# Column halves for the large loads of a half chunk, and a new set of priorities, in a planned recurrence and gated feed-forward kernel

## The chip, the core and the metric

One core of a Trainium2 chip. The metric is the device time of one execution in microseconds, the median of several runs. Engines: TensorE (PE in the profile, its weight loads PEld), VectorE (DVE), ScalarE (ACT), GpSimd (POOL) and SyncE (SP), which issues every transfer of this kernel through one queue, in order. Sixteen DMA engines move the bytes.

## What is computed

Two parts, one after the other: a recurrence over 768 tokens for 4 batches and 8 heads of width 40, and a gated feed-forward layer on its output.

```python
for t in range(S):                                   # S = 768
    y[:, :, t] = einsum('bhd,bhde->bhe', r_t, state)
    Sa = einsum('bhde,bhe->bhd', state, a_t)
    state = state * w_t - einsum('bhd,bhe->bhde', Sa, b_t) + einsum('bhd,bhe->bhde', v_t, k_t)
x = y as 3072 rows of 320
out = ((x @ w_a) * (x @ w_b)) @ w_out                # w_a, w_b 320 x 1536, w_out 1536 x 320
```

## The kernel before

The tokens are cut into 12 chunks of 64 (C), and the 32 pairs of batch and head into two halves (c = 0, 1) of 16; a "half chunk" is one c of one chunk n. For each chunk the recurrence becomes matrix work:

- `prep(n, c, v)` (one half chunk, independent of the state). It loads W (decays) and BA, a row of 1536 numbers: columns 0 to 1023 hold b and k (BK), columns 1024 to 1535 hold a (A). DVE makes running products of the decays (two scans into Q, the reciprocal d between them), multiplies BK and A by them, PE makes the scores (`at<-BA`) and transposes BK (`at<-ident,BA`), ACT stores the scores of one kind into AB, DVE those of the other into TK. TK, A and part of Q go to a scratch row in memory, `un_d[q]`, from which `main` reads them.
- `lanes(g, v, halved)` (a group of one or two chunks: 0; 1 and 2; 3 and 4; ...). A triangular solve on DVE: transpose N, then steps that each are a product Yt and a sum Y, then two transposes, TC and T. For the first two groups `halved` shortens the steps (14 pairs instead of 30), and `join` on PE and ACT puts the halves together. `merge` makes of it the matrix T of each chunk.
- `main(n, v)` (the chain over the chunks). It loads ak and pt (both from `un_d`), SV (v by tokens) and RV (r in its first half, v in its second, by channels), then runs a chain on PE with ACT and DVE between: `r_` (`at<-SV,ak`), `u_` and `ut_` (`at<-RH,T`, `at<-T,RH`), `s_` (`at<-SV,bn`, the new state ST), `g_` (`at<-rv`, masked by DVE into G: `G<-at,tri`), `y_` (`at<-rv,SD`, `at<-G,bn`). `pack` lays the result out as xk, the input of the feed-forward layer.
- The feed-forward weights come as 64-bit words. They are cut into 12 slices of 128 columns, each of three pieces (w_a, w_b, w_out). `decode` turns a piece into a high and a low part by a chain of small steps that alternates between ACT, DVE and POOL, through two raw buffers and one pair of temporaries, so the pieces go one after the other. The slices 0 to 5 (F1) are decoded while the first chunks run; the `sc` entry of WG starts them after the scores of half chunk 1. `unit` is one slice on one chunk: 16 matmuls `ab<-xk,wt`, a product g by ACT and DVE, 6 matmuls `po<-wo`. Slices 0 to 5 are done chunk by chunk beside the recurrence, slices 6 to 11 at the end, on two chunks at a time (`at<-xk,wt`, 512 columns).

What sets the order: every step is recorded in a `Plan` with its engine, a length, what it reads and writes, and a priority v. `Plan.run` then lays the steps out in time by its own table of lengths, and at each point an engine takes, of the steps that could begin, the one with the smallest v. The instructions are issued in that order, and on the chip each engine runs its own in that order, waiting wherever an input is late. So priorities, lengths and dependencies set the order on every engine at once.

The priorities are simple sums. With rank the first chunk of a group:

```python
prep(n, c, rank[n] + PV + PV1 * (n - rank[n]) + 0.1 * c)
wv = [WV + WV1 * f if f < F1 else NS - 3 + 0.3 * (f - F1) for f in range(NSL)]
lanes(g, g[0] + LV if g[0] else LV0, halved)
join(n, x, n + MV);  merge(g, g[0] + MV);  main(n, n);  units of chunk n: n + UV + f / F1
```

Before: the preps of chunk 0 have -2.99 and -2.89, those of chunk 1 have -1.99 and -1.89, the solve of chunk 0 has -1.85 (LV0), and the weight slices 0 to 5 have -4.44 to -3.64. A transfer is a step of SP with a number of microseconds for its bytes; the plan also holds that a transfer is issued only when the eighth transfer before it has landed.

Of the kernel before, what the change touches and what calls it, by code (L numbers as in the profile page):

```python
# [23 lines left out]
C = 64  # L24
# [3 lines left out]
NP = 2  # L28
# [27 lines left out]
SMALLEST = 0.5 / (1.125 * 2.0 ** -15)  # L56
PV, PV1, LV, MV, UV, WV, WV1 = -2.99, 0.43, -0.68, -1.45, 1.44, -4.44, 0.16
LV0 = -1.85
LIMIT = 2.0 ** 8
# [274 lines left out]
def wkv_moe(ctx, tc, wd, ba, rvf, vn, pin, rv, wa, wb, wo, out):  # L334
# [310 lines left out]
    def prep(n, c, v):  # L645
# [26 lines left out]
        load(lambda: (W, wd[n, c]), n, [], [kW], 0.75)  # L672
        load(lambda: (BA, ba[n, c]), n, [], [kBK, kA], 2.5)

# [236 lines left out]
    def main(n, v):  # L911
# [9 lines left out]
        for c, q in enumerate(qs):  # L921
            vc = v + 0.1 * c
            pl.dma(lambda q=q: nc.sync.dma_start(out=AK_[q % NU], in_=un_d[q][:, 0:AW]),
                   [("un", q, i) for i in (0, 1, 3, 4)] + begun(n), [kU[c]], 1.65, v=vc - 0.3)
            load_v(n, c, vc - 0.2)
            load(lambda c=c: (RV_[c].rearrange("p x m t -> p (x m t)"), rvf[n, c]), n, begun(n), [kRV[c]], 1.7, v=vc - 0.2)
            pl.dma(lambda q=q: nc.sync.dma_start(out=PT_[q % NU], in_=un_d[q][:, AW:]), [("un", q, 2)] + begun(n), [kP[c]], 0.85, v=vc - 0.1)
# [10 lines left out]
        def r_(ps=ps):  # L938
            for c in both:
                for i in range(4):  # L940
                    for gq in range(2):
                        for j in range(2):
                            k = mi(gq, i) * D
                            mul(bank(ps, c)[half(j), k:k + D], AK[c][:, gq, j, i], SV[:, c, gq, j, i])
        pl.op("PE", 1.86, r_, ["svs", *kV, *kU], [("r", n), "rh"], need=ps, work=2560, mode="cc", lat=0.1)
        for c in both:
# [65 lines left out]
        for c in both:  # L1012
            ps = Banks(2)

            def g_(c=c, ps=ps):
                for m in range(M):
                    for kind in range(2):
                        for gq in range(2):
                            l = RV_[c][hd(gq), 1, m] if kind else UT[hd(gq), c, m]
                            mul(bank(ps, gq)[half(gq ^ kind), m * C:(m + 1) * C], l, RV_[c][hd(gq), 0, m])  # L1020
            pl.op("PE", 0.98, g_, [("ut", 0), ("ut", 1), kRV[c]], [("gs", n, c), ("gm", c, 0), ("gm", c, 1)], need=ps, work=1280, mode="qq", lat=0.1, v=v + 0.1)
            for gq in range(2):
                pl.op("DVE", us(512), lambda c=c, gq=gq, ps=ps: nc.vector.tensor_mul(
                    out=G[:, c, gq].rearrange("p j i t -> p (j i) t"), in0=bank(ps, gq).rearrange("p (m t) -> p m t", t=C),
                    in1=tri[:, None, :].to_broadcast([P, M, C])), [("gs", n, c)],
                    [("gm", c, gq)] + ([("xf", 0, x) for x in range(4)] if c else ["x"]), free=[(ps, gq)], v=v + 0.1)
# [3 lines left out]
        def y_(ps=ps):  # L1030
# [8 lines left out]
            for c in both:  # L1039
                for gq in range(2):  # L1040
                    for i in range(4):
                        for j in range(2):
                            c0 = (c * 4 + i) * C
                            mul(bank(ps, gq)[hd(j), c0:c0 + C], BN[c][:, mi(gq, i), j], G[:, c, gq, j, i], not n, True)
        pl.op("PE", 2.9 if n else 2.1, y_, [("gm", c, x) for c in both for x in range(2)] + [*kBN, *kRV] + [("sd", c) for c in both],
              [("y", n), "x"], need=ps, work=6144, mode="qc" if n else "cc", lat=0.1, v=v + 0.2)
# [164 lines left out]
    class Later:  # L1211


        def __init__(self, s, i):
            self.s, self.i = s, i

    keys_a = ([(k, i) for k in ("U", "pt") for i in range(NU)] + [("bn", i, k) for i in range(NBN) for k in range(2)] + [("T", i, k) for i in range(NT) for k in range(3)]
              + [(k, c) for k in ("svv", "rv", "sd", "ut") for c in range(NP)] + ["svs", "rh", "st", "x"]
              + [("gm", c, x) for c in range(NP) for x in range(2)] + [("xf", 0, i) for i in range(4)] + ["judge"])
# [282 lines left out]
```

## Time and profile before

| | |
|---|---|
| median of 3 runs (lowest, highest) | 752.42 us (749.15, 755.53) |
| the profiled execution | 752.64 us |
| its span, first to last instruction | 750.9 us |
| granted TensorE clock, mean over the span | 0.916 |
| busy: PE, DVE, ACT, POOL | 673.7, 539.2, 400.8, 230.1 us |
| moved by the transfers | 117.11 MB in 68692 packets |

Busy time counts what an engine executes; issuing transfers and waiting on semaphores are not counted. The chain of waits is followed back from the last instruction, at each step to what released it. "issue" is time in which an engine waited for nothing that the profile shows. All work issued through the planner shows line 75, so groups are told apart by tiles. The clock is given as a share of 2.4 GHz: 1.00 is 2.4 GHz, 0.50 is 1.2 GHz.

### The profile page before, as it was taken

To read this page: it belongs to the slowest core of one execution; us is meant where nothing else is said; L and a number is where in the kernel's file an instruction comes from. 1 tells how busy PE (TensorE), PEld (TensorE's weight loads), DVE (VectorE), ACT (ScalarE), POOL (GpSimd) and SP (SyncE) were. 2 spreads that over 40 slices of the span, in tenths; PEclk is the share of its full clock that TensorE was granted. 3 is DMA by queue.
4 is the path that set the end of the run, shared out by engine and by line. 5 is a ranking of instruction groups with operands and counts; after the bars stand their busy time and mean duration, and the time that the engine had idled before them with its cause. 6 is when DMAs were issued, how large, how long until landed. Compare 5 with 4: busy or idle time off the path is not lost.

```text
span 750.9 us, 29601 instructions
## 1 busy us (share of the span) xinstructions
PE 673.7 (90%) x12997; PEld 619.3 (82%) x12997; DVE 539.2 (72%) x992; ACT 400.8 (53%) x898; POOL 230.1 (31%) x236
## 2 busy tenths in 40 slices
PE   5446765997999998999999999999999999999996
PEld 3435654897999988989899999899998888888886
DVE  8999998889688995999789998466374444322133
ACT  5547667475663575556746545586475344312221
POOL 5034444341001121211211111266375465522220
PEclk8556666598999998999999999999999999999998
DMA  7998698146685685667656617383841111000112
GB/s 221 316 294 247 162 297 237 50 129 203 195 263 171 200 263 167 184 200 201 217 167 183 204 40 207 100 225 114 256 133 52 43 39 38 3 1 4 67 71 75
DMA packets 68692, 117.11 MB, mean 156 GB/s; under 512 B 6796, under 2 KB 46764, under 8 KB 68556
## 3 DMA queue, kind: packets, MB, share of 16 engines
q1 hardware_dynamic: 68556, 115.14, 52.0%
q8 instruction: 104, 1.70, 1.0%
q14 instruction: 32, 0.26, 0.1%
HBM read 76.91 MB, written 32.80 MB: 146 GB/s over the span
## 4 chain that ended last, share of the span: by engine, by line
PE 79%; DVE 11%; issue 5%; DMA 3%; SPq 1%; POOL 1%; ACT 1%; DVEq 0%; POOLq 0%
PE at L75 41%; PE ab L75 24%; PE po L75 13%; DVE Q L75 2%; DVE Y L75 1%; DVE Yt L75 1%; DVE BA L75 1%; DMA ak<-un_d 1%; DMA wraw<-in_wb_dram 1%; DVE G L75 1%; DVE w_ex L75 1%; DMA wraw<-in_wo_dram 1%; SPq L75 1%; DVE TC L75 1%; DVE TK L75 1%
## 5 line engine op out<-in xcount | busy, mean ns | idle before, releaser
L75 PE MATMUL ab<-xk,wt 120*128 120x256 f32 x1216 | 171.0, 294 | 0.0
L75 PEld LDWEIGHTS ab<-xk,wt 120*128 120x128 f32 x1216 | 157.9, 198 | 2.8 <-issue 0.2
L75 PE MATMUL at<-xk,wt 120*128 120x512 f32 (+1 forms) x576 | 132.1, 381 | 0.0
L75 POOL TENSOR_TENSOR gl<-g,gh 128x256 fp32r<-128x256 f32 x66 | 59.4, 902 | 230.8 <-ACT gh L75 202.4
L75 PEld LDWEIGHTS at<-xk,wt 120*128 120x128 f32 x576 | 102.9, 188 | 19.1
L75 PE MATMUL po<-wo,gh 128*128 128x320 f32 x312 | 85.4, 324 | 0.7 <-issue 0.7
L75 DVE TENSOR_TENSOR m<-at,m 128x512 f32<-128x512 f32 x32 | 22.1, 691 | 85.3 <-PE at L75 83.1
L75 DVE TENSOR_TENSOR Yt<-Y,N 128x112 f32<-128x112 f32 (+22 forms) x173 | 70.1, 405 | 4.0
L75 DVE TENSOR_TENSOR Y<-Y,Yt 128x112 f32<-128x112 f32 (+22 forms) x173 | 65.3, 377 | 5.9
L75 POOL TENSOR_TENSOR w_mt<-w_mt,w_ex 120x384 f32<-120x384 f32 (+1 forms) x33 | 36.0, 1090 | 94.1 <-ACT w_mt L75 93.2
L75 POOL TENSOR_TENSOR m<-m,m 128x512 fp32r<-128x512 f32 x32 | 41.7, 1303 | 75.4 <-ACT m L75 75.2
L75 ACT COPY g<-ab 128x256 f32<-128x256 f32 x76 | 28.2, 371 | 62.0 <-PE ab L75 59.1
L75 PEld LDWEIGHTS po<-wo,gh 128*128 128x128 f32 x312 | 56.4, 191 | 2.5 <-issue 0.9
L75 DVE TENSOR_TENSOR g<-ab,g 128x256 f32<-128x256 f32 x76 | 31.7, 417 | 32.8 <-ACT g L75 32.5
L75 ACT CAST m<-m 128x512 fp32r<-128x512 f32 x32 | 19.9, 621 | 58.7 <-DVE m L75 57.0
L75 DVE TENSOR_TENSOR BA<-BA,Q 128x1024 f32<-128x1024 f32 (+1 forms) x48 | 48.9, 1038 | 0.1
L75 PE MATMUL po<-wo,gl 128*128 128x320 f32 x156 | 48.8, 313 | 0.0
L75 PE MATMUL at<-BA 64*64 64x64 f32 x1536 | 36.0, 252 | 12.4 <-issue 9.3
L75 PEld LDWEIGHTS at<-BA 64*64 64x64 f32 x1536 | 31.9, 163 | 16.2 <-issue 10.9
L75 ACT CAST gh<-g 128x256 fp32r<-128x256 f32 x80 | 32.4, 406 | 22.1 <-DVE g L75 20.2
L75 PE MATMUL at<-ident,BA 104*128 104x104 f32 x192 | 27.2, 285 | 15.6 <-DVE BA L75 7.8
L75 ACT ACTIVATE AB<-at 32x256 f32<-32x256 f32 (+1 forms) x72 | 32.4, 450 | 15.0 <-PE at L75 13.8
(122 smaller groups left out, 1363.5 us busy)
## 6 DMA issues: line engine op xcount, KB each, us to landing
BA<-in_ba_dram SPq DMA_DIRECT2D x22, 672.0 KB
ak<-un_d SPq DMA_DIRECT2D x24, 512.0 KB
rv<-in_rvf_dram SPq DMA_DIRECT2D x22, 448.0 KB
un_d<-Q SPq DMA_DIRECT2D x24, 260.0 KB
pt<-un_d SPq DMA_DIRECT2D x24, 260.0 KB
un_d<-BA SPq DMA_DIRECT2D x48, 128.0 KB
un_d<-TK SPq DMA_DIRECT2D x48, 128.0 KB
x_d<-G SPq DMA_DIRECT2D x12, 512.0 KB
```

The source lines that it names most:

```text
L75: r = fn(*args, **kwargs)
```

## The change

Three loads are issued as two transfers of half the columns or of the two parts (BA in 1024 and 512 columns, RV and ak in 512 and 512), each half with a key of its own in the plan, and eight priorities have new values.

```diff
-PV, PV1, LV, MV, UV, WV, WV1 = -2.99, 0.43, -0.68, -1.45, 1.44, -4.44, 0.16
-LV0 = -1.85
+PV, PV1, LV, MV, UV, WV, WV1 = -3.05, 0.55, -0.63, -1.25, 1.35, -4.72, -1.4
+LV0 = -4.93
...
-        load(lambda: (BA, ba[n, c]), n, [], [kBK, kA], 2.5)
+        load(lambda: (BA[:, 0:2 * M * C], ba[n, c][:, 0:2 * M * C]), n, [], [kBK], 1.67)
+        load(lambda: (BA[:, 2 * M * C:], ba[n, c][:, 2 * M * C:]), n, [], [kA], 0.83)
...
-            pl.dma(lambda q=q: nc.sync.dma_start(out=AK_[q % NU], in_=un_d[q][:, 0:AW]),
-                   [("un", q, i) for i in (0, 1, 3, 4)] + begun(n), [kU[c]], 1.65, v=vc - 0.3)
+            for g in range(2):
+                ag = slice(g * AW // 2, (g + 1) * AW // 2)
+                pl.dma(lambda q=q, ag=ag: nc.sync.dma_start(out=AK_[q % NU][:, ag], in_=un_d[q][:, ag]),
+                       [("un", q, i) for i in (0, 1, 3, 4)] + begun(n), [(*kU[c], g)], 0.83, v=vc - 0.3)
             load_v(n, c, vc - 0.2)
-            load(lambda c=c: (RV_[c].rearrange("p x m t -> p (x m t)"), rvf[n, c]), n, begun(n), [kRV[c]], 1.7, v=vc - 0.2)
+            for x in range(2):
+                load(lambda c=c, x=x: (RV_[c][:, x].rearrange("p m t -> p (m t)"), rvf[n, c][:, x * M * C:(x + 1) * M * C]),
+                     n, begun(n), [(*kRV[c], x)], 0.85, v=vc - 0.2)
...
-        pl.op("PE", 1.86, r_, ["svs", *kV, *kU], [("r", n), "rh"], need=ps, work=2560, mode="cc", lat=0.1)
+        pl.op("PE", 1.86, r_, ["svs", *kV, *((*k, g) for k in kU for g in range(2))], [("r", n), "rh"], need=ps, work=2560, mode="cc", lat=0.1)
...
-            pl.op("PE", 0.98, g_, [("ut", 0), ("ut", 1), kRV[c]], [("gs", n, c), ("gm", c, 0), ("gm", c, 1)], need=ps, work=1280, mode="qq", lat=0.1, v=v + 0.1)
+            pl.op("PE", 0.98, g_, [("ut", 0), ("ut", 1), (*kRV[c], 0), (*kRV[c], 1)], [("gs", n, c), ("gm", c, 0), ("gm", c, 1)], need=ps, work=1280, mode="qq", lat=0.1, v=v + 0.1)
...
-        pl.op("PE", 2.9 if n else 2.1, y_, [("gm", c, x) for c in both for x in range(2)] + [*kBN, *kRV] + [("sd", c) for c in both],
+        pl.op("PE", 2.9 if n else 2.1, y_, [("gm", c, x) for c in both for x in range(2)] + [*kBN, *((*k, 0) for k in kRV)] + [("sd", c) for c in both],
```

With the new values the solve of chunk 0 stands at -4.93, the preps of chunk 0 at -3.05 and -2.95, those of chunk 1 at -2.05 and -1.95, and the weight slices 0 to 5 at -4.72, -6.12 and so on down to -11.72. The raw buffers keep the pieces in their old order. The key of a's part lets the first half of an RV load (r, read by `g_` and `y_`) and the second (v, read by `g_` alone) come free at different steps.

What the change makes of the order, at three places.

VectorE at the start, from the second TK product of chunk 0 (`TK_182`; `Q_178`, `BA_179` belong to chunk 1, `w_mt` to the first weight piece, N, AB, Y and Yt to the solve of chunk 0). Before:

```order
L75 TENSOR_TENSOR TK_182<-at_63,tri 128x512
L75 SCALAR_TENSOR_TENSOR Q_178<-W_176,one 128x521
L75 RECIPROCAL d_183<-Q_178 128x8
L75 SCALAR_TENSOR_TENSOR Q_178<-W_176,d_183 128x520
L75 STREAM_TRANSPOSE N<-AB 128x32x32
L75 TENSOR_TENSOR AB<-AB,off 128x16x32
L75 TENSOR_TENSOR BA_179<-BA_179,Q_177 128x1024
L75 TENSOR_SCALAR w_mt_162<-wraw_159 120x384
L75 TENSOR_TENSOR BA_179<-BA_179,Q_177 128x512
L75 COPY Y<-N 128x2x15
```

and now:

```order
L75 TENSOR_TENSOR TK_182<-at_63,tri 128x512
L75 STREAM_TRANSPOSE N<-AB 128x32x32
L75 TENSOR_TENSOR AB<-AB,off 128x16x32
L75 COPY Y<-N 128x2x15
L75 TENSOR_TENSOR Yt<-Y,N 128x56
L75 TENSOR_TENSOR Y<-Y,Yt 128x2x2x14
```

The scans, the products of chunk 1 and all weight steps have left the solve; it runs through without a break, and the first weight step stands right behind its last transpose.

VectorE where the first chunk's chain reaches G (`ST` and `G<-at,tri` belong to main(0); Y and Yt now to the solve of chunks 1 and 2). Before:

```order
L75 TENSOR_TENSOR Yt<-Y,N 128x128
L75 TENSOR_TENSOR Y<-Y,Yt 128x2x8x8
L75 TENSOR_TENSOR ST<-at_66,pcs 128x8x40
L75 TENSOR_TENSOR ST<-at_65,pcs 128x8x40
L75 TENSOR_TENSOR Yt<-Y,N 128x126
L75 TENSOR_TENSOR Y<-Y,Yt 128x2x9x7
L75 TENSOR_TENSOR G<-at_64,tri 128x512
```

and now:

```order
L75 TENSOR_TENSOR ST<-at_63,pcs 128x8x40
L75 TENSOR_TENSOR ST<-at_65,pcs 128x8x40
L75 TENSOR_TENSOR AB<-AB,off 128x16x32
L75 TENSOR_SCALAR w_mt_162<-wraw_159 120x384
L75 TENSOR_TENSOR TK_181<-at_64,tri 128x512
L75 TENSOR_TENSOR G<-at_65,tri 128x512
L75 TENSOR_TENSOR BA_180<-BA_180,Q_178 128x512
L75 TENSOR_TENSOR G<-at_63,tri 128x512
L75 COPY Y<-N 128x2x15
```

Eight pairs of solve steps and the copy Y, which stood ahead of the first G, now stand behind the second; beside them one product of BA_180, one `w_mt`, two `w_ex` of each kind have moved behind G too.

TensorE between `g_` and `y_` of chunk 2 (`wt_224` is slice 0, `wt_226` slice 1, `wt_228` slice 2, `wt_234` and `wo_235` slice 5). Before:

```order
L75 MATMUL at_65<-rv_205 64x64
L75 MATMUL ab_68<-xk,wt_234 128x256 x8
L75 MATMUL ab_67<-xk,wt_224 128x256 x16
L75 MATMUL at_65<-rv_204,SD_210 40x64
L75 MATMUL at_66<-rv_204,SD_210 40x64
```

and now:

```order
L75 MATMUL at_65<-rv_205 64x64
L75 MATMUL ab_67<-xk,wt_228 128x256 x16
L75 MATMUL ab_68<-xk,wt_226 128x256 x8
L75 MATMUL po_69<-wo_235,gh_166 128x320
L75 MATMUL po_69<-wo_235,gl_168 128x320
L75 MATMUL po_69<-wo_235,gh_166 128x320
L75 MATMUL po_70<-wo_235,gh_166 128x320
L75 MATMUL po_70<-wo_235,gl_168 128x320
L75 MATMUL po_70<-wo_235,gh_166 128x320
L75 MATMUL at_65<-rv_204,SD_210 40x64
```

What moved is feed-forward work: counted from the start of the program to the `y_` of chunk 2, PE now has 136 `ab` matmuls, 36 `po` and 472 of the preps' matmuls, where it had 112, 30 and 440; the counts of the solves and of the main chain are the same. Up to the first `ab` the only difference is one set of 32 score matmuls that now stands ahead of it.

## Rows read from the trace of the kernel before

**Rows 1.** The page, part 1 and the clock line of part 2.

```profile
PE 673.7 (90%) x12997; PEld 619.3 (82%) x12997; DVE 539.2 (72%) x992; ACT 400.8 (53%) x898; POOL 230.1 (31%) x236
...
PEclk8556666598999998999999999999999999999998
```

**Rows 2.** Stages: length, busy PE, PEld, DVE, ACT, POOL; clock, DMA share, GB/s.

```profile
16.40:47.70 31.30, 11.93 (x209) 10.12 (x209) 28.90 (x63) 15.00 (x34) 1.00 (x1) 0.55 1.00 297
47.70:87.90 40.20, 25.70 (x944) 23.04 (x948) 39.37 (x61) 27.86 (x61) 20.07 (x16) 0.67 0.86 241
87.90:121.50 33.60, 23.50 (x784) 20.86 (x774) 32.26 (x52) 22.38 (x48) 17.01 (x14) 0.61 0.83 239
121.50:157.20 35.70, 29.52 (x903) 27.76 (x895) 28.89 (x57) 21.28 (x46) 11.24 (x11) 0.70 0.37 106
157.20:184.00 26.80, 22.06 (x614) 20.33 (x615) 25.97 (x56) 18.10 (x42) 8.17 (x8) 0.99 0.75 219
```

**Rows 3.** VectorE in order of time: start, length, instruction.

```profile
19.00 2.06 DVE L75 STREAM_TRANSPOSE N<-AB 128x1024 f32<-128x1024 f32 x1
...
45.82 1.91 DVE L75 STREAM_TRANSPOSE T<-Y 128x1024 f32<-128x1024 f32 x1
...
87.89 0.69 DVE L75 TENSOR_TENSOR G<-at,tri 128x512 f32<-128x512 f32 x1
```

**Rows 4.** TensorE's waits for "issue", 121.5 to 184 us: total, times, longest.

```profile
PE at L75 <- issue: 9.6, 5, 3.1
```

**Rows 5.** VectorE's groups, 75.2 to 87.8 us: count, busy, mean ns, idle before.

```profile
L75 DVE TENSOR_TENSOR Y<-Y,Yt 128x126 f32<-128x126 f32 (+6 forms) x8 | 4.3, 541 | 0.3
L75 DVE TENSOR_TENSOR Yt<-Y,N 128x126 f32<-128x126 f32 (+6 forms) x8 | 2.9, 364 | 0.2
...
L75 DVE COPY Y<-N 128x30 f32<-128x30 f32 x1 | 1.0, 976 | 0.0
```

**Rows 6.** VectorE's groups by form, 0 to 207 us.

```profile
L75 DVE TENSOR_TENSOR_SCAN Q<-W,one 128x521 f32<-128x521 f32 x14 | 18.8, 1342 | 0.0
...
L75 DVE TENSOR_TENSOR BA<-BA,Q 128x512 f32<-128x512 f32 x13 | 10.5, 804 | 0.0
...
L75 DVE SCALAR_TENSOR_TENSOR w_ex<-wraw,w_ex 120x384 f32<-120x384 uint32 x12 | 6.7, 558 | 0.4
...
L75 DVE STREAM_TRANSPOSE TC<-Y 128x1024 f32<-128x1024 f32 x3 | 6.2, 2083 | 0.1
...
L75 DVE TENSOR_SCALAR w_ex<-w_mt 120x384 int32<-120x384 int32 x12 | 4.1, 345 | 1.0 <-POOL w_mt L75 0.9
```

**Rows 7.** VectorE's solve sums by line, 16.4 to 47.7 us.

```profile
L75 DVE TENSOR_TENSOR Y<-Y,Yt 128x56 f32<-128x56 f32 (+7 forms) x14 | 3.6, 260 | 0.5
```

**Rows 8.** ScalarE in order of time: the copies of one half chunk's scores into AB.

```profile
119.31 1.39 ACT L75 ACTIVATE AB<-at 128x512 f32<-128x512 f32 x3
```

**Rows 9.** Chain of waits, in order of time: start, length, engine and tile.

```profile
136.99 3.71 PE ab L75 x16
...
209.53 1.93 PE ab L75 x16
...
211.46 0.88 PE po L75 x6
```

**Rows 10.** TensorE in order of time: scores of a half chunk, first matmuls of slice 5.

```profile
158.55 1.33 PE L75 MATMUL at<-BA 64*64 64x64 f32 x64 [0.18 <-DVE G L75]
...
176.91 1.21 PE L75 MATMUL ab<-xk,wt 120*128 120x256 f32 x8
```

**Rows 11.** GpSimd in order of time: the last step on slice 5's second piece.

```profile
164.86 1.01 POOL L75 TENSOR_TENSOR wt<-w_mt,w_ex 120x384 fp32r<-120x384 f32 x1
```

**Rows 12.** VectorE's first step on each weight piece: ns (least, median, most), first and last start.

```profile
L75 DVE TENSOR_SCALAR w_mt<-wraw x18: 294/332/360, 23.0 to 167.4; 120x384 int32<-120x384 int32 x12, 128x320 int32<-128x320 int32 x6
```

**Rows 13.** Transfers: SP's issues of BA (ns, least, median, most), and the page's queue line.

```profile
L75 SPq DMA_DIRECT2D BA<-in_ba_dram x24: 312/398/1454, 1.3 to 389.2; - x24
...
q1 hardware_dynamic: 68556, 115.14, 52.0%
```

More of the change, by code (lines that the diff above doesn't have):

```diff
@@ L1215, in __init__ @@
             self.s, self.i = s, i
-    keys_a = ([(k, i) for k in ("U", "pt") for i in range(NU)] + [("bn", i, k) for i in range(NBN) for k in range(2)] + [("T", i, k) for i in range(NT) for k in range(3)]
-              + [(k, c) for k in ("svv", "rv", "sd", "ut") for c in range(NP)] + ["svs", "rh", "st", "x"]
+    keys_a = ([("pt", i) for i in range(NU)] + [(k, i, g) for k in ("U", "rv") for i in range(NU) for g in range(2)] + [("bn", i, k) for i in range(NBN) for k in range(2)] + [("T", i, k) for i in range(NT) for k in range(3)]
+              + [(k, c) for k in ("svv", "sd", "ut") for c in range(NP)] + ["svs", "rh", "st", "x"]
               + [("gm", c, x) for c in range(NP) for x in range(2)] + [("xf", 0, i) for i in range(4)] + ["judge"])
```

## The prediction

> **What bounds the kernel now.** I read four views in this order: the page's busy times and clock, a table of stages, VectorE's instructions in order of time, and TensorE's waits with the chain of waits. The page shows TensorE busy for 673.7 of 750.9 us and a clock at half speed in parts of the first quarter and nearly full behind it [rows 1]. So the end is TensorE's, and it can only come earlier if TensorE idles less, or runs less at half clock. The table of stages says where that can be: of the 77.2 us idle, 31.30 - 11.93 = 19.4 lie between 16.4 and 47.7 us, 14.5 between 47.7 and 87.9, 10.1 up to 121.5, 6.2 up to 157.2 and 4.7 up to 184 [rows 2]. In these stages the engine that is full is VectorE: 28.90 of 31.30, 39.37 of 40.20 and 32.26 of 33.60 us in the first three [rows 2]. From 121.5 us, where the first feed-forward matmul stands, this changes: VectorE is busy for 28.89 of 35.70, and of TensorE's 10.9 idle us up to 184 9.6 are "issue", waits that no other engine ends [rows 2, 4]. So up to 121.5 us whatever VectorE does ahead of the first chunk's result delays TensorE; from there on TensorE is paced by its own work, and what counts is how much of it has been done by a given point.
>
> **The change part by part.** The new order matters by what VectorE no longer does ahead of three points.
>
> The first point is the end of the first solve. It began at 19.00 and its last transpose ended at 45.82 + 1.91 = 47.7 us [rows 3]; VectorE was busy for 28.90 us in that stretch, and the solve itself is 14 sums of 3.6 us together, 14 products about as long, and three transposes, near 14 us in all [rows 2, 3, 6, 7]. The other 15 us now stand behind it, so T is due at 32 to 33 us. This isn't a gain by itself: the 15 us are chunk 1's products and weight pieces, most of which still stand ahead of the first G.
>
> The second point is the first G, at 87.89 us [rows 3]. Ahead of it are missing now eight pairs of solve steps and a copy, 4.3 + 2.9 + 1.0 = 8.2 us [rows 5]; half a product of BA, 0.80; one w_mt, 0.33; two w_ex of each kind, 2 x (0.345 + 0.558) = 1.81 [rows 6, 12]: 11.1 us at these lengths. The sums here took 541 ns each, against 260 ns in the first solve [rows 5, 7]; at 260 ns a step the 16 steps are 4.2 us, and the whole is 7.1. One wait is added: the transpose N needs both half chunks' scores in AB, three copies of 1.39 us together [rows 8], and the scans that stood between are gone. It costs at least nothing and at most those 2.7 us (two scans of 1.34); I take 0.8. Queued behind it on VectorE are the solve and chunk 1's prep. So G should come 6 to 10 us earlier.
>
> The third point decides: the feed-forward input of chunk 0 and the first `ab` at 121.5 us. Ahead of the xk step are missing one scan, 1.34, its reciprocal, some 0.2 (an estimate, it does 8 numbers), half a product of BA, 0.80, one w_mt and the two pairs of w_ex, 0.33 + 1.81: 4.5 us [rows 6, 12]. Less 0.8 for N this is 3.7 us. TensorE has also done one set of scores more by then, 1.33 us [rows 10], which was idle time put to use: the first `ab` comes about 2.4 us earlier, and TensorE stands 3.7 us better.
>
> A check further on, at chunk 2's G and y_: missing on VectorE are one transpose TC, 2.08, and three short solve steps, at most 0.36 each [rows 5, 6]; added are half a BA product, 0.80, one product by tri, 0.69 like G [rows 3], and one g of half that width. Net 2.8 - 1.9 = 0.9, less 0.8 for N: VectorE gets there at the old time. But TensorE has by then done 24 `ab` more, 24 x 1.93 / 16 = 2.9, six `po`, 0.9 (0.88 for six), and the scores, 1.33 [rows 9, 10]: 5.1 us of work that otherwise comes later, and the 4.7 us idle in that stage can take only what is not "issue". So the two points say 3.7 and 5.2 us. Behind chunk 2 TensorE has the same work in both, and the counts meet again at chunk 7; I take 4.5 us.
>
> The split itself: 72 loads become 144, so 72 more issues of 0.40 us [rows 13], 29 us on SP in all; by the order, 109 issues instead of 93 lie ahead of chunk 0's result, 6.4 us. Each SP wait holds up the transfers queued behind it. I cost them at nothing, because the first solve gives VectorE 14 us that need no transfer; uncovered they would be up to 6.4. The rows of data grow by 24 x 128 for ak and 2 x (22 x 112 + 2 x 128) for BA and RV, 8512 in all; at the mean 0.52 x 16 x 750.9 / 68556 = 91 ns per packet [rows 13] and 16 engines that is at most 48 us of transfer time over the whole span, at least none if time goes by bytes. I take none: 297 GB/s at a share of 1.00 and 241 at 0.86 (280 at full) differ little [rows 2]. Nothing is gained by the two halves of ak, which wait for the same stores.
>
> The Trainium skill speaks against this part: "DMA: Bandwidth & Descriptors", section "Rules for kernel authors", wants 1 MiB or more per transfer, since each carries a fixed cost of about 2 us. By it the first ak load would land some 2 us later (my estimate from that page), and the forecast would be about 750 us. The trace shows the queue full from 16.4 to 47.7 us with transfers under 1 MB at 297 GB/s [rows 2], so a fixed cost overlaps there.
>
> Sum: 752.6 of the profiled execution (span 750.9 and 1.7 around it) less 4.5 gives 748.1, which is 0.6% under the median of 752.4; the execution profiled is a typical one.
>
> **The rivals.** *The clock rises earlier.* Between 121.5 and 157.2 us the granted clock is 0.70, though TensorE is busy for 29.52 us [rows 2]: a slice costs 3.71 us of `ab` there and 1.93 later [rows 9]. With work packed more closely a half-clock stretch could end sooner. If the two slices and the six `po` that ran slowly there ran at full clock, that is 2 x 1.78 + 0.7 = 4.3 us more: 743.8. Against it: up to the first `ab` TensorE has the same work in nearly the same order, only earlier.
>
> *Transfers take VectorE's place.* The queue is full from 16.4 to 47.7 us and at 0.86 up to 87.9, that is 31.3 + 34.6 = 65.9 us of 71.5 [rows 2]. Chunk 0's loads, chunk 1's and 2's stay ahead of its G, so G can come 5.6 us earlier at most, and any time per packet takes from that. Up to 121.5 us there are 5.7 us more of room. The added rows ahead of chunk 0's result (10 loads of BA, 4 of ak, 4 of RV) are 2144; at half the mean packet, 2144 x 46 ns / 16 = 6.1 us, the 4.5 us are gone: 752.
>
> *Slower: the weights come late.* The pieces go one behind the other through two raw buffers. The first solve now runs ahead of the first piece, which starts on VectorE 8 us later by the lengths, and slice 5's second piece is 7 us later. Before, its last step ended at 165.9 us and the slice's first matmul stood at 176.9 [rows 10, 11]; now it would end near 173, and the fill of its last rows follows, while the matmul, which has moved to chunk 2's `g_`, is due near 180. 7 us are left. If the chain slips by more than 7 us, TensorE waits in its queue with chunk 2's `y_` behind it, and from 11.5 us on the kernel is slower than before. The 18 pieces follow each other every (167.4 - 23.0) / 17 = 8.5 us [rows 12]; a slip of two, 17 us, gives 752.6 + 17 - 11.5 = 758.1. For it: all pieces now outrank everything but the solve, so little can hold them up; that speaks against it.
>
> **How the numbers follow.** The forecast has 0.5, the clock 0.2, the transfers 0.2, the late weights 0.1. The forecast's own range is 746 to 750.5 (2 to 6.5 us, from the 3.7 and 5.2 and what the wait for N can cost or spare). The range for eight in ten goes from the clock rival with the larger of the two gains, 752.6 - 5.2 - 4.3 = 743.1, a little further for both VectorE prices of the second point, to 740.5, and up to 757, most of the late weights' case. A measurement of this kernel can tell about 1%, 7.5 us, from no change. Faster by more than that, under 744.9, is most of the clock rival and the low end of the forecast: 0.24. Slower, over 759.9, is a long slip of the weights: 0.07. The rest is 0.69.
>
> **What would show it.** Right: the last transpose, T, ended at 32 to 33 us, the first G at 78 to 82, the first `ab` at 118 to 120, idle TensorE up to 184 us near 50 us instead of 55. In the table of stages the time from there on must be as before. The clock rival shows as a stage near 130 to 150 us at full clock; the transfers as VectorE waits on loads between 30 and 80 us, which were 1 us before; the late weights as TensorE waiting for POOL or SP's fill ahead of a slice's first `ab`. The forecast is wrong if the first `ab` doesn't move, or if it does and the end stays.

## The result, and the profile after

| | before | changed |
|---|---|---|
| median, first comparison (20 runs each) | 750.16 us | 743.0 us (737.03 to 756.26) |
| median, second comparison (29 and 12 runs) | 750.39 us | 745.81 us (742.13 to 752.23) |
| profiled execution: span, TensorE busy, mean clock | 750.9, 673.7 us, 0.916 | 737.2, 664.2 us, 0.935 |
| a second profile of the changed kernel | | 741.1, 672.2 us, 0.922 |

The ratio was 0.9905 [0.9876, 0.9935] in the first comparison and 0.9973 [0.9937, 1.0009] in the second (e6 below). It is formed from the undisturbed runs alone; the medians are of all runs. The medians differ by 7.2 and 4.6 us. By the ratios the gain is 7.1 and 2.0 us; the two intervals don't overlap, and the second reaches no change. The forecast was 748.1 us, 4.5 less than before, with 746 to 750.5 as its own range and 740.5 to 757 for eight in ten: the medians lie 3.0 and 0.2 us below the first range and inside the second.

The mean granted clock of the runs behind the ratio was 0.926 in the first comparison and 0.919 in the second; before had 0.920 in the second, and 0.918 or 0.919 in three others. Among the changed kernel's first 20 runs one with a clock lower by 0.01 is some 4 to 5 us longer (an estimate, a straight line through them), so 0.007 is some 3 us, most of what the two comparisons differ by. At before's clock the changed kernel is thus faster by some 2 to 4 us; whether the higher clock of the first comparison is the order's doing isn't shown.

The two profiles of the changed kernel show 13.7 and 9.8 us less than that of before, more than either pair of medians. The executions profiled make the excess: they took 738.91 and 742.82 us, 4.1 and 3.0 under the medians of the changed kernel, and the one of before took 752.64, 2.5 over its median of 750.16.

The page of the changed kernel, parts 1 to 3, for [rows 1] and the queue line of [rows 13]:

```profile
PE 664.2 (90%) x12997; PEld 609.6 (83%) x12997; DVE 541.3 (73%) x992; ACT 400.1 (54%) x898; POOL 230.5 (31%) x236
...
PEclk8577758998999989999999999999999999999998
...
q1 hardware_dynamic: 78220, 115.15, 52.3%
```

The eighth digit of the clock, 129 to 147 us, is 9 where before has 5 [rows 1]. TensorE idles 73.0 us instead of 77.2, and is busy 9.5 us less with the same 12997 matmuls, at a mean clock of 0.935 instead of 0.916. The queue carries 9664 packets more in the same bytes at the same share, 52.3% of a shorter span.

The table of stages of the changed kernel (columns as in [rows 2]), first profile:

```profile
16.40:47.70 31.30, 14.40 (x529) 12.17 (x529) 29.46 (x61) 14.03 (x32) 1.11 (x2) 0.56 0.93 262
47.70:87.90 40.20, 26.63 (x807) 24.54 (x808) 38.88 (x62) 31.21 (x70) 16.84 (x13) 0.79 0.93 274
87.90:121.50 33.60, 20.06 (x757) 17.69 (x757) 32.02 (x51) 19.76 (x44) 18.59 (x14) 0.59 0.77 217
121.50:157.20 35.70, 31.17 (x990) 29.00 (x978) 34.38 (x68) 25.61 (x57) 12.28 (x12) 0.95 0.56 164
157.20:184.00 26.80, 22.53 (x531) 20.73 (x530) 26.01 (x54) 16.11 (x38) 9.17 (x8) 0.87 0.61 189
```

and the same stages in the second profile:

```profile
16.40:47.70 31.30, 14.28 (x529) 12.05 (x529) 28.80 (x61) 13.10 (x30) 1.10 (x2) 0.55 0.92 256
47.70:87.90 40.20, 27.28 (x800) 25.23 (x800) 39.26 (x60) 31.35 (x70) 17.53 (x13) 0.75 0.92 271
87.90:121.50 33.60, 19.00 (x668) 16.48 (x669) 31.98 (x52) 19.70 (x44) 18.50 (x14) 0.62 0.78 223
121.50:157.20 35.70, 33.98 (x1007) 32.17 (x1006) 28.77 (x62) 21.76 (x49) 11.14 (x12) 0.69 0.45 133
157.20:184.00 26.80, 22.07 (x496) 20.13 (x496) 25.57 (x52) 17.83 (x41) 10.18 (x9) 0.94 0.77 214
```

The row to compare is the fourth. The same program ran at a clock of 0.95 there in one execution and at 0.69 in the other, where before had 0.70 [rows 2]. A busy TensorE at 0.69 isn't more work: 33.98 us against 31.17.

VectorE in order of time, the changed kernel, first profile:

```profile
16.70 2.07 DVE L75 STREAM_TRANSPOSE N<-AB 128x1024 f32<-128x1024 f32 x1 [0.29 <-ACT AB L75]
...
29.82 1.87 DVE L75 STREAM_TRANSPOSE T<-Y 128x1024 f32<-128x1024 f32 x1
...
78.17 0.69 DVE L75 TENSOR_TENSOR G<-at,tri 128x512 f32<-128x512 f32 x1 [0.56 <-PE at L75]
```

T ended at 31.7 us instead of 47.7, and the first G stands at 78.17 instead of 87.89 [rows 3]; the wait for AB, which the change adds at N, is 0.29 us, and the second profile shows none. TensorE, first profile:

```profile
118.42 1.21 PE L75 MATMUL ab<-xk,wt 120*128 120x256 f32 x8
...
129.00 3.68 PE L75 MATMUL ab<-xk,wt 120*128 120x256 f32 x16
...
135.75 2.08 PE L75 MATMUL ab<-xk,wt 120*128 120x256 f32 x16
```

and the second:

```profile
119.56 1.97 PE L75 MATMUL ab<-xk,wt 120*128 120x256 f32 x8
...
131.44 3.78 PE L75 MATMUL ab<-xk,wt 120*128 120x256 f32 x16
...
140.47 3.46 PE L75 MATMUL ab<-xk,wt 120*128 120x256 f32 x16
```

The first `ab` comes at 118.4 or 119.6 us; before it was 121.5. In the first profile the second whole slice runs in 2.08 us, at full clock; in the second it takes 3.46 us, and before it was 3.71 us for a slice there [rows 9].

An account at 184 us, from the pages and from one line of each profile: before, the changed kernel twice, and then two runs from below, e4 (the order of before) and e7 (the new order up to chunk 2):

```profile
0.00:184.00 184.00, 122.75 (x3580) 108.54 (x3584) 169.75 (x298) 113.53 (x250) 68.52 (x76) 0.71 0.75 220
0.00:184.00 184.00, 124.83 (x3740) 110.58 (x3741) 175.10 (x307) 115.67 (x259) 69.02 (x76) 0.77 0.77 227
0.00:184.00 184.00, 126.74 (x3649) 112.31 (x3649) 168.74 (x297) 112.97 (x252) 69.48 (x76) 0.72 0.77 224
0.00:184.00 184.00, 122.52 (x3611) 106.45 (x3614) 170.82 (x298) 112.94 (x250) 69.09 (x76) 0.73 0.77 220
0.00:184.00 184.00, 128.65 (x3727) 113.77 (x3728) 172.13 (x305) 114.43 (x256) 69.96 (x76) 0.73 0.78 226
```

Taken from the whole, TensorE's busy time that is left behind this point is 551.0 us before, 539.4 in the first profile and 545.5 in the second; its idle time behind it is 15.9, 13.8 and 11.6 us. (The busy time left holds the half-clock stretches behind that point.) So these two executions get there 11.6 or 5.5 us ahead, and save 2.1 or 4.3 us of idle time afterwards. Since they were quicker than their kernel's median, the fairer pair is e4 and e7, whose profiled executions lie within 1 us of their medians, at clocks of 0.73 up to 184 us in both: 550.0 and 542.9 us of work left, 14.7 and 15.8 us idle behind. There the new order is 7.1 us ahead at 184 us and loses 1.1 afterwards.

### The profile page after: what moved, and what is told of

Its sections match the earlier page's. It is cut to its first block, busy times and chain, and to the rows that moved or that the text cites. A ratio compares the mean times of both kernels' runs of the same rounds, so it can differ in the third digit from the quotient of the medians.

```text
span 737.2 us, 29754 instructions
## 1 busy us (share of the span) xinstructions
PE 664.2 (90%) x12997; PEld 609.6 (83%) x12997; DVE 541.3 (73%) x992; ACT 400.1 (54%) x898; POOL 230.5 (31%) x236
## 2 busy tenths in 40 slices
DMA packets 78358, 117.13 MB, mean 159 GB/s; under 512 B 7948, under 2 KB 47916, under 8 KB 78220
## 3 DMA queue, kind: packets, MB, share of 16 engines
q1 hardware_dynamic: 78220, 115.15, 52.3%
## 4 chain that ended last, share of the span: by engine, by line
PE 79%; DVE 10%; issue 4%; ACT 3%; DMA 2%; SPq 1%; POOL 1%; DVEq 0%; POOLq 0%; ACTq 0%
PE at L75 42%; PE ab L75 23%; PE po L75 13%; DVE Yt L75 2%; DVE Y L75 2%; DMA ak<-un_d 1%; SPq L75 1%; DVE BA L75 1%; DMA x_d<-G 1%; DVE G L75 1%; ACT w_ex L75 1%; DVE Q L75 1%; ACT AB L75 1%; DVE w_ex L75 0%; POOL w_mt L75 0%
## 5 line engine op out<-in xcount | busy, mean ns | idle before, releaser
L75 PE MATMUL ab<-xk,wt 120*128 120x256 f32 x1216 | 167.3, 289 | 0.7 <-DVE xk L75 0.7
L75 PEld LDWEIGHTS ab<-xk,wt 120*128 120x128 f32 x1216 | 153.6, 192 | 3.6 <-DVE xk L75 0.9
L75 DVE TENSOR_TENSOR Y<-Y,Yt 128x112 f32<-128x112 f32 (+22 forms) x173 | 68.3, 395 | 5.9
L75 DVE TENSOR_TENSOR Yt<-Y,N 128x112 f32<-128x112 f32 (+22 forms) x173 | 68.1, 394 | 4.3
L75 ACT COPY g<-ab 128x256 f32<-128x256 f32 x76 | 28.2, 372 | 65.8 <-PE ab L75 60.1
L75 ACT CAST gh<-g 128x256 fp32r<-128x256 f32 x80 | 32.4, 406 | 21.6 <-DVE g L75 17.8
L75 ACT ACTIVATE AB<-at 32x256 f32<-32x256 f32 (+1 forms) x72 | 32.4, 450 | 11.9 <-PE at L75 10.7
L75 ACT COPY m<-at 128x512 f32<-128x512 f32 x32 | 18.7, 583 | 35.7 <-PE at L75 35.5
L75 PE MATMUL at<-T,AB 32*32 32x32 f32 x1152 | 19.7, 205 | 20.4 <-DVE T L75 18.0
L75 POOL TENSOR_TENSOR w_mt<-w_mt,wt 120x384 f32<-120x384 f32 x22 | 27.2, 1238 | 34.2 <-DVE w_ex L75 13.1
```

The source lines that it names most:

```text
L75: r = fn(*args, **kwargs)
```

## The experiments

Theory A, as in the prediction: the priorities make the gain, by what VectorE no longer does ahead of the first chunk's result; the split is free. Rival B: the split makes it. Rival C: any new order shifts the half-clock stretches, and that is all. After the first four runs A was replaced by R and Q (below). In one table, from the profiles (first `ab`, first G of chunk 1, span, and TensorE's busy time left and idle time behind 184 us) and from the comparisons with before:

| kernel | first `ab` | chunk 1's G | span | busy left / idle behind 184 us | median | ratio to before, 95% |
|---|---|---|---|---|---|---|
| before | 121.5 | 157.2 | 750.9 | 551.0 / 15.9 | 750 to 754 | 1 |
| changed | 118.4 | 147.1 | 737.2 | 539.4 / 13.8 | 743.0 | 0.9905 [0.9876, 0.9935] |
| e1 split only | 121.7 | 155.9 | 757.8 | 551.6 / 22.2 | 757.78 | 1.0103 [1.0049, 1.0157] |
| e2 priorities only | 122.7 | 163.7 | 762.9 | 558.7 / 20.2 | 766.37 | 1.0231 [1.0174, 1.0287] |
| e3 first solve only | 108.9 | 168.1 | 772.9 | 564.0 / 24.9 | 774.76 | 1.0332 [1.0275, 1.0389] |
| e4 cut, same order | 123.4 | 157.1 | 748.7 | 550.0 / 14.7 | 749.8 | 0.9993 [0.9956, 1.003] |
| e5 joined | 123.2 | 155.5 | 854.7 | 598.7 / 72.0 | 854.25 | 1.1421 [1.1351, 1.1491] |
| e6 changed, again | 119.6 | 151.0 | 741.1 | 545.5 / 11.6 | 745.81 | 0.9973 [0.9937, 1.0009] |
| e7 new, then old | 120.0 | 148.3 | 742.6 | 542.9 / 15.8 | 743.39 | 0.9939 [0.9911, 0.9966] |
| e8 padded before | 122.1 | 154.5 | 755.5 | 553.0 / 18.5 | 755.37 | 1.0057 [1.0013, 1.0102] |
| e9 e2, preps later | 97.7 | 159.5 | 761.7 | 559.0 / 18.7 | 760.58 | 1.0148 [1.0094, 1.0203] |
| e10 some joined | 120.6 | 149.7 | 742.5 | 543.2 / 15.3 | 749.22 | 1.0007 [0.9968, 1.0046] |
| e11 changed, preps later | 100.0 | 150.9 | 750.2 | 546.9 / 19.3 | 755.19 | 1.0079 [1.0049, 1.0109] |
| e12 old, then new | 123.0 | 155.0 | 761.6 | 554.8 / 22.8 | 763.51 | 1.0145 [1.0087, 1.0203] |

**e1, the split alone.** The changed kernel with the old values:

```diff
-PV, PV1, LV, MV, UV, WV, WV1 = -3.05, 0.55, -0.63, -1.25, 1.35, -4.72, -1.4
-LV0 = -4.93
+PV, PV1, LV, MV, UV, WV, WV1 = -2.99, 0.43, -0.68, -1.45, 1.44, -4.44, 0.16
+LV0 = -1.85
```

> The loads are split as in the changed kernel, all eight priorities are the old ones. Theory A (the priorities make the gain, the split is free and brings nothing): between -2 and +2 us against before; the last transpose T near 45 us, the first G near 86 us, the first ab at 119.5 to 122 us, a long half-clock stretch behind it as before. Theory B (the split makes the gain, since a step can begin on half a load): -4 to -9 us. Theory C (neither by itself: any new order shifts the half-clock stretches behind the first ab, and that makes the time): the time follows the length of the half-clock stretches from 110 to 210 us, whichever sign.

It is 1.0% slower, where A allowed 2 us either way and B a gain. C had either sign, by the half-clock stretches; but from 110 to 210 us the clock was 0.88 here, 0.80 in before and 0.84 in e4, which called for a faster kernel. So C isn't all there is, and B falls. The halves have keys of their own, so the plan makes another order of them even with the old priorities. Two stages of it:

```profile
207.00:240.00 33.00, 30.25 (x701) 27.97 (x701) 26.31 (x51) 16.23 (x40) 3.55 (x4) 0.90 0.83 253
...
300.00:360.00 60.00, 55.22 (x1382) 51.69 (x1380) 52.06 (x105) 30.43 (x71) 7.74 (x10) 0.94 0.62 186
```

At 184 us it stands as before (551.6 us of work left instead of 551.0). It loses later, 22.2 us of idle time behind that point instead of 15.9: 2.8 us from 207 to 240 and 4.8 from 300 to 360, where before idled 0 and 1.7.

**e2, the priorities alone**, and **e3, the first solve alone**, both with whole loads:

```diff
-LV0 = -1.85
+LV0 = -4.93
```

is all of e3; e2 has all eight new values.

> Whole loads as before, all eight new priorities. Theory A: -4 to -9 us against before, T ends at 32 to 33 us, the first G at 76 to 80 us (11 us less of VectorE's work stands ahead of it), first ab at 118 to 120.5 us. Theory B: -2 to +2 us. Theory C: the time follows the half-clock stretches from 110 to 210 us.

> Whole loads, old priorities but for the solve of chunk 0 (LV0 = -4.93). Theory A, with the first solve as its one cause: -4 to -9 us; T at 32 to 33 us, first G at 76 to 80, first ab at 115 to 118 us (VectorE has 5 to 6 us less ahead of the first chunk's result). If the other seven priorities are what counts: -2 to +3 us although the first ab is earlier. Theory B: -2 to +2. Theory C: by the half-clock stretches.

Both are slower, by 2.3 and 3.3%, outside what A and B allowed, and e3 is the kernel that does what theory A asks for: T at 32.4, G at 78.7 and the first `ab` at 108.9 us, 12.6 us ahead of before. TensorE's rows at that point in e3:

```profile
108.90 0.80 PE L75 MATMUL ab<-xk,wt 120*128 120x256 f32 x2
110.33 1.23 PE L75 MATMUL ab<-xk,wt 120*128 120x256 f32 x4 [0.64 <-DVE xk L75]
```

Its chunk 1 reaches G at 168.1 us, 10.9 us behind before. So an early first `ab` is not enough (busy time left behind 184 us: 564.0), and A falls as a general rule. In e2, VectorE's waits from 47.7 to 87.9 us and its scans up to chunk 2's G:

```profile
DVE TK L75 <- PE at L75: 5.0, 2, 3.2
```

```profile
L75 DVE TENSOR_TENSOR_SCAN Q<-W,d 128x520 f32<-128x520 f32 x15 | 20.4, 1357 | 0.5
L75 DVE TENSOR_TENSOR_SCAN Q<-W,one 128x521 f32<-128x521 f32 x15 | 19.7, 1312 | 1.6 <-ACT Q L75 1.6
```

VectorE waits 5 us for scores (in the changed kernel's first profile all its waits in that stretch are 0.6 us, at G), and 30 scans stand ahead of chunk 2's G, where the changed kernel and before have 24: 40.1 us of scans instead of 32.6 and 32.7, the rest for later chunks. That gave theory Q (VectorE's work ahead of the G of chunks 1 and 2 decides), tried in e9 and e11, and theory R: split and priorities act only through the order that the plan makes of both, and the transfers as such are neutral.

**e4, the split without a new order.** Before, each large load issued as two transfers inside the same step:

```diff
+            cut = {1536: 1024, 1024: 512}.get(out.shape[-1])
+            if cut:
+                nc.sync.dma_start(out=out[:, 0:cut], in_=src[:, 0:cut])
+                out, src = out[:, cut:], src[:, cut:]
             nc.sync.dma_start(out=out, in_=src)
```

(and ak likewise).

> The kernel before with its order on every engine unchanged; each load of BA, ak and RV is issued as two transfers, one right behind the other, inside the same step. This prices the split alone. Theory A: -1 to +1 us, share of the transfer queue within 1 point of 52.0%, SP busy issuing for some 29 us more off the path. Rows cost time (91 ns each over 16 engines): up to +6 us. Theory B with halves landing earlier: at most -2 us, since every reader here still stands where it stood.

Its page: the queue line, with as many packets as in the changed kernel (9664 more than before; the prediction's sum had 8512).

```profile
q1 hardware_dynamic: 78220, 115.15, 52.4%
```

Ratio 0.9993 [0.9956, 1.003], share 52.4% of 748.7 us: as a transfer, in the old order, the split costs and brings nothing that can be measured. First G and first `ab` came 3 and 2 us later than in the profile of before, and one of the two slices behind ran at full clock (2.17 us, the other 3.39).

**e5 and e10, the new order with whole loads.** Where a load's halves meet, one whole transfer in the place of the second:

```diff
+    def pair(self, first, second, whole):
...
+        def one():
+            first.held = go
+        def two():
+            if first.held:
+                first.held = None
+                whole()
+            else:
+                second.go()
```

> The changed kernel with its order on every engine but SP unchanged; where the two halves of a load stand together and nothing reads the first between, one whole transfer is issued in the place of the second (all 24 of ak, 13 of 24 of BA, chunk 0's RV; nearly all that bear on the first 150 us). Theory R, formed on the first four runs (split and priorities act only through the order that the plan makes of both; the halves as transfers bring nothing): within 2 us of the changed kernel, -5 to -9 us against before. Rival S (the shorter transfers themselves help, since instruction fetches and other loads wait less behind them): TensorE's issue waits rise from 20 to 24 us or more and the gain shrinks to -3 us or less.

e5 is 14% slower instead of 5 to 9 us faster, and says nothing on the question: where halves did not meet (22 of RV, 11 of BA), the first half was held back until just ahead of its first reader. What it prices is a late load. Its longest waits on transfers:

```profile
DVE BA L75 <- DMA BA<-in_ba_dram: 56.7, 15, 7.3
...
PE at L75 <- DMA rv<-in_rvf_dram: 43.8, 17, 3.8
```

e10 is the mended form, which joins only halves that stand directly one behind the other:

> e5 mended: the changed kernel with its order unchanged, and one whole transfer only where the plan issues the two halves directly one behind the other (all 24 of ak, 5 of BA, chunk 0's first RV: 30 of 72); every other half is issued where it was. Theory R (shorter transfers bring nothing by themselves): within 3 us of the changed kernel, -3 to -9 us against before. Rival S (they do): -2 us or less, with more issue waits of TensorE than 17 to 20 us.

Its profile is that of the changed kernel (span 742.5, chunk 1's G at 149.7 us), its 10 runs are not: ratio 1.0007, where R wanted 3 us less at the least. TensorE's issue waits were 22.4 us in all, against 20.2 and 18.7 in the two profiles of the changed kernel. The time is what S expected, and R's range is missed. The issue waits say little, since before and e4, with one order, differ by 4.5 us in them (26.5 and 22.0). The interval overlaps that of the second comparison (0.9973) and not that of the first (0.9905). Whether the shorter transfers are worth nothing in the new order, or anything up to some 7 us, stays open.

**e6, the changed kernel again.**

> The changed kernel once more, for a second profile of the same program. Ratio to before 0.987 to 0.994 as measured. If the half-clock stretches differ from execution to execution, this profile has one of another length between 120 and 160 us (3.4 us in the first), and its span is longer by about half of what that stretch is longer; without such a difference the span is within 2 us of 737.2 and the medians' 7 us must be read against the profile's 13.7 in another way.

The ratio, 0.9973, missed the 0.987 to 0.994 that were expected; the profile did show another half-clock stretch, and a longer span with it. The stages were shown above. Around the stretch in question, before:

```profile
130.00:151.00 21.00, 18.75 (x474) 17.94 (x477) 18.51 (x42) 10.40 (x22) 5.97 (x6) 0.53 0.21 54
```

the changed kernel's first profile:

```profile
130.00:151.00 21.00, 19.42 (x645) 17.91 (x646) 20.21 (x45) 12.91 (x29) 7.37 (x7) 0.94 0.36 106
```

and its second:

```profile
130.00:151.00 21.00, 21.00 (x500) 20.18 (x495) 16.23 (x41) 12.26 (x27) 6.23 (x6) 0.68 0.27 79
```

In the same 21 us TensorE gets through 645 instructions at 0.94 and through 500 at 0.68. The second span is 3.9 us longer, and chunk 1's G comes 3.9 us later. So that stretch is worth about 4 us between these two, and it differs between executions of one program. It doesn't follow that the order has no part in it: profiles with the order of before up to here show 0.53, 0.70 (e4) and 0.71 (e12) from 130 to 151 us, those with the new order 0.94, 0.68, 0.88 (e7) and 0.96 (e10). These are too few to tell.

**e7 and e12, where the gain lies.** Each priority carries two values, and the plan changes over when it issues chunk 2's `y_`:

```diff
-                    x[1].v + (STAY if e == "PE" and x[1].mode[0] != last else 0.0), x[1].seq))
+                    (x[1].v if not isinstance(x[1].v, Two) else x[1].v.b if self.then else x[1].v.a) + (STAY if e == "PE" and x[1].mode[0] != last else 0.0), x[1].seq))
...
         def y_(ps=ps):
+            pl.then = pl.then or n == 2
```

> The changed kernel up to the y_ of chunk 2 (near 185 us), word for word; from there on the plan goes by the eight old priorities. Theory R with all of the gain made ahead of that point: -4 to -10 us against before. If the order of the later chunks carries part of it: -3 us or less, with TensorE's idle time or half clock up between 200 and 535 us.

> The mirror of e7: the kernel before, whole loads, word for word up to the y_ of chunk 2 (near 190 us); from there on the plan goes by the eight new priorities. Theory R (the gain is made ahead of that point, the later order is worth nothing): -3 to +3 us against before. If the new values pay in the later chunks too: -4 us or less. If they only fit split loads: +4 us or more.

e7 keeps the gain (0.9939), as R expected: with the old values from chunk 2 on, the kernel is as fast as the changed one. TensorE has 542.9 us of work left behind 184 us, between the changed kernel's two profiles. What the change gains, it has gained by then, or by the clock (0.925 in these runs, before 0.920). The mirror, e12, is 1.5% slower and not the same, as was expected if the new values only fit split loads: even with before up to 300 us, it then falls back, and idles 22.8 us behind 184 us instead of 15.9:

```profile
360.00:420.00 60.00, 55.72 (x1239) 52.73 (x1229) 48.51 (x100) 31.68 (x76) 9.37 (x10) 0.94 0.59 176
420.00:470.00 50.00, 47.44 (x1217) 44.94 (x1216) 42.32 (x91) 24.90 (x57) 6.99 (x10) 0.93 0.42 124
```

Here it idles 4.3 and 2.6 us, at a clock that was 1.00 in before. So R's "the later order is worth nothing" holds for the pairs of e7 and the changed kernel only; another later order costs 10 us.

**e8, a direct trial of the clock.** Before, with ten matmuls more whose results nothing reads:

```diff
+    def fill(n):
+        for _ in range(n):
+            mul(PO[0].rearrange("p (m t) -> p m t", t=HB), fl, eye[:, None, :].to_broadcast([P, NP * M, HB]))
...
         def t3(ps=ps):
+            fill(4 if n == 2 else 0)
...
         def tc_(ps=ps2):
+            fill(4 if n == 2 else 0)
...
         def l2a(ps=ps):
+            fill(2 if g[0] == 1 else 0)
```

> The kernel before with ten more matmuls of 512 columns on TensorE, whose results are not used, ahead of three steps of chunk 2 between 123 and 132 us (four, four, two), where TensorE waits on issue for 6 us. Clock theory (the half-clock stretch from 130 to 151 us follows on a TensorE that idles ahead of it, and costs 3 to 4 us): granted clock 1.00 from about 134 us on, -1 to -5 us against before. Rival (the clock there doesn't follow what TensorE does just ahead, or the pads only come on top): the stretch stays, +2 to +6 us.

```profile
130.00:151.00 21.00, 19.27 (x635) 17.64 (x633) 20.04 (x43) 15.84 (x34) 6.48 (x7) 0.92 0.25 62
...
360.00:370.00 10.00, 8.42 (x110) 8.34 (x109) 4.73 (x6) 4.80 (x12) 0.73 (x1) 0.66 0.39 109
```

The clock half of the theory came as expected, in one execution: 0.92 from 130 to 151 us, where the three profiles of this order without pads had 0.53 to 0.71, and chunk 1's G 2.7 us earlier in spite of the ten matmuls. As the changed kernel had 0.94 and 0.68 there without any pads, this doesn't show that the pads did it. The end did not come: 0.6% slower, some 4 us, which is what the rival expected. From 177 us on TensorE waited 4.46 us for "issue" in the middle of chunk 2's `g_` (2.96 in before, at the same place), the clock stood at half behind it, as in before, and around 365 us it fell once more, where before had full clock. The pads are ten matmuls more, with their weight loads, in TensorE's queue, and what that does to the waits for "issue" (28.2 us in all, before 26.5) wasn't separated from the clock:

```profile
181.81 0.37 PE L75 MATMUL at<-rv,uT 40*64 40x64 f32 x2 [4.46 <-issue]
```

**e9 and e11, theory Q.** One line each, in e2 (0.2) and in the changed kernel (0.4):

```diff
-                prep(n, c, rank[n] + PV + PV1 * (n - rank[n]) + 0.1 * c)
+                prep(n, c, rank[n] + PV + PV1 * (n - rank[n]) + 0.1 * c + (0.2 if n > 2 else 0.0))
```

> Whole loads and all new priorities, as in e2_prio_only, and the preps of the chunks from 3 on 0.2 later in priority. In the order of e2 six scans more than in the changed kernel (30 against 24) stand on VectorE ahead of chunk 2's G, with a transpose and products, some 15 us in all; with the 0.2 it is 24 again. Theory Q (the new priorities lose by VectorE's work ahead of the G of chunks 1 and 2, not by the whole loads as transfers): 10 to 18 us faster than e2, that is -4 to +6 us against before, chunk 2's G at 180 to 192 us instead of 207.7. Rival (a whole load comes late in the new order, wherever the preps stand): within 4 us of e2, +10 us or more against before.

> The changed kernel, with the preps of the chunks from 3 on 0.4 later in priority. By the order VectorE has some 2, 9 and 10 us less ahead of the G of chunks 0, 1 and 2 than in the changed kernel, 3 us less at chunk 3, and about as much feed-forward work done. Theory Q: chunk 1's and 2's G 6 to 10 us earlier, and 3 to 8 us faster than the changed kernel, -8 to -15 us against before. Rival (from the first ab on TensorE is paced by its own work, so an earlier G gains nothing there): within 2 us of the changed kernel.

e9 put chunk 2's G at 191.3 us, inside what was expected, and recovered some 6 us of e2's loss (1.0231 to 1.0148), not 10 to 18; at 11 us over before it lies where the rival had it. It has the earliest `ab` of all, 97.7 us, and is still 1.5% slower than before; from 121.5 to 157.2 us it ran at

```profile
121.50:157.20 35.70, 27.89 (x854) 26.38 (x844) 25.95 (x51) 22.04 (x49) 10.80 (x11) 0.57 0.41 114
```

a clock of 0.57, with 7.8 us idle. e11 missed at both ends: chunk 1's G came no earlier (150.9 us, VectorE busy for 24.73 of 35.70 us there, so no longer the limit), and the late preps then held up the last chunk, where TensorE waits for VectorE's g and the last xk:

```profile
520.00:540.00 20.00, 15.86 (x95) 14.26 (x93) 11.77 (x19) 12.47 (x29) 12.57 (x13) 0.91 0.86 232
540.00:560.00 20.00, 18.98 (x105) 16.89 (x106) 13.15 (x22) 12.27 (x27) 11.94 (x11) 0.91 0.61 169
```

5.2 us idle where the changed kernel idles 0. So Q is at most one term of e2's loss, about a third, and no rule. No version here beats the changed kernel; e7's ratio lies between its two.

## Why the prediction came out, point by point

**The number.** Part of the agreement is luck. The forecast started from an execution of 752.6 us, taken as typical, where the longer series have medians of 750.2 and 750.4; its gain of 4.5 us lies between the 7.1 and 2.0 us that the two comparisons gave, and the difference between these two goes with the clock, which the sum had left out.

**The first solve and the first G.** T was due at 32 to 33 us and ended at 31.7; G was due at 78 to 82 and stood at 78.2, 78.3 and 78.8 in the three profiles that share this beginning. The count of instructions in the order, at the lengths of [rows 5 to 8, 12], held to about a microsecond at T and lies at the early end at G. The added wait at N was 0.29 us at most instead of 0.8.

**The first `ab`.** Due at 118 to 120, seen at 118.4, 119.6 and 120.0. The step is right, but what was hung on it is not general: in e3, e9 and e11 the first `ab` came 13 to 24 us earlier than before, and all three are slower. Here chunk 1's G came earlier too, by 6 to 10 us, which the prediction had not worked out. That is no rule either: e11 has it 6.3 us earlier and is slower, with 5.2 us idle near its end.

**TensorE's state at chunk 2.** The check at chunk 2's `y_` gave 5.1 us of work done ahead, and 4.5 us was taken. Measured at 184 us it is 5.5 us in the profile whose clock was as low as before, 11.6 in the first profile, and 7.1 between e4 and e7. Idle TensorE from 16.4 to 184 us was to be near 50 instead of 55: 52.8 and 51.0 us in the two profiles, 49.4 in e7, and 55.9 in e4 with the old order. This is the step that carried the forecast. It came in the direction and near the size forecast; how much of these microseconds is the order's and how much the clock's isn't separated.

**"From there on as before".** Not quite: behind 184 us TensorE idled 2.1 and 4.3 us less, nearly all of it issue waits, 7.6 and 5.5 us instead of 10.2. I had counted none of this. It may be the execution's: in e7, with the other later order, idle time behind 184 us is as before (15.8 and 15.9 us), and e10, with the later order of the changed kernel, has 15.3.

**The clock.** I set it up as a rival at 4.3 us. Its size was right (3.9 us between two executions of one program), and what was to show it, a stage near 130 to 150 us at full clock, is there in the first profile (0.94) and not in the second (0.68). Its form was wrong: it is not another outcome of the change but a term that comes and goes, and before has it too, since in e4 with the order of before one of the two slow slices ran at full clock. Whether the new order makes it come more often isn't shown. The argument against it ("the same work in nearly the same order") was no argument.

**The rivals on transfers and weights.** Neither came. The transfers were to let G come 5.6 us earlier at most, and it came 9.7 earlier. All of VectorE's waits from 16.4 to 121.5 us in the changed kernel's first profile, none of them for a load (nor is any in the second):

```profile
DVE w_mt L75 <- POOL wt L75: 0.8, 1, 0.8
DVE G L75 <- PE at L75: 0.6, 1, 0.6
DVE N L75 <- ACT AB L75: 0.3, 1, 0.3
```

Ahead of an `ab` TensorE waits 0.7 us in all (1.2 in the second profile), for xk, and never for a weight piece.

**The split at nothing.** Right as a transfer in the old order (e4), open in the new one (e10). As information for the plan it is not nothing: alone it costs 1.0%, and without it the new values cost 2.3%. The prediction spoke of the priorities and the split as two parts with a price each; they have only one price together. Its sum was made on the order of the finished kernel and not on the edits, so it needed no price of either part. Nor are all eight values alive: with LV, or with WV and WV1, at their old value the plan gives the same program, so what the rival on late weights said of pieces that "now outrank everything" was no change at all.

**The Trainium skill's rule** in "DMA: Bandwidth & Descriptors", section "Rules for kernel authors", wants 1 MiB or more per transfer for the full bandwidth. The 2 us that the prediction names with it stand in another section of that page of the Trainium skill, fitted on transfers that GpSimd issues, while here SyncE issues them; no view here shows when a half landed. By the Trainium skill's rule the split should have cost time in the queue, and the trace doesn't agree: 52.4% of 748.7 us in e4 with 78220 packets, 52.0% of 750.9 before with 68556, ratio 0.9993.

**Open:** which of the moves ahead of chunk 2 is the one that pays. Each trial that changed one of them made another order of everything behind it, so none was seen by itself.

## What to carry to other kernels

When a planner sets the order, read the finished order and count what each engine does ahead of several points down the chain, at two or three chunks and not only at the first result; the edits themselves have no price of their own. Take a second profile of the same program before explaining differences of half a per cent: here two executions of one program were 3.9 us apart with a clock of 0.95 and 0.69 in one stage, and two comparisons of the same pair of kernels gave 0.9905 and 0.9973. Cutting the loads in two cost no measurable time here in an unchanged order, but a split must be judged with the order that follows from it.

## What the runs showed of the hardware

- One program, two executions: the granted clock from 121.5 to 157.2 us was 0.95 and 0.69. With ten unused matmuls ahead of 130 us (e8) it was 0.92 from there to 151 us, in three profiles of that order without them 0.53 to 0.71; in e8 a wait of 4.46 us was followed by half clock.
- The mean clock of a run goes with its time: 0.925 and 743.6 us, the means of the changed kernel's 20 runs in the first comparison, 0.919 and 746.4 us, those of its 12 in the second.
- TensorE's waits for "issue" differ between orders of the same instructions, from 14.2 us (e5) and 18.7 (e6) to 30.8 (e2), without a visible releaser; before has 26.5, and e4, whose order is that of before, 22.0.
- Cutting 72 transfers of 448 to 768 KB in two added 9664 packets and no measurable time in an unchanged order (e4); a transfer issued only just ahead of its reader (e5, 33 of 72) cost 104 us.
